# Gathers of later experts paced by the blocks of the expert in work

## The chip, the cores and the metric

The kernel runs on one core of a Trainium2 chip. The metric is the device time of one execution in microseconds (us); the smaller the better. Engines are named as in the profile: PE is TensorE (PEld its weight loads), DVE is VectorE, ACT is ScalarE, POOL is GpSimd, SP is SyncE, which issues the plain DMA transfers.

## What is computed

Attention with a local band of 96 keys and 8 global keys over q, k, v of shape (4, 8, 768, 64), then a mixture of eight experts in which each of the 3072 tokens goes to the one expert with the largest gate logit, with no token dropped:

```python
x = attn_out.transpose(0, 2, 1, 3).reshape(3072, 512)
logits = x @ w_gate                                # (3072, 8)
expert_idx = argmax(logits, axis=1)
gate_w = softmax(logits)[arange(N), expert_idx]
for e in range(8):
    lo, hi = boundaries[e], boundaries[e + 1]      # the tokens of expert e, sorted by expert
    h = maximum(x_sorted[lo:hi] @ w1[e], 0.0)      # w1[e]: 512 x 1024
    y_sorted[lo:hi] = h @ w2[e]                    # w2[e]: 1024 x 512
out = gate_w[:, None] * y_sorted[inv_perm]
```

All is float32.

## The kernel before

The first part, to about 230 us, is the attention, the gating and the sorting of tokens. It writes the attention's rows x into a DRAM tensor `x_tok` in pieces of 128 numbers. While it ends, the first 256 tokens of expert 0 are already worked on (`work`). Then each expert is worked on for as many tokens as its capacity says. The experts after 0 are taken in the order of their load, and position p below is the place in this order:

```python
CAPS = (464, 416, 416, 400, 400, 368, 368, 272)
ORDER = (0, 1, 2, 3, 4, 7, 5, 6)      # position 5 has capacity 272, positions 6 and 7 have 368
```

An expert's rows are brought from `x_tok` by indirect DMAs that GpSimd issues, one for 32 tokens (128 pieces of 512 bytes), into one of two buffers `xq_s`. VectorE then turns them in squares of 32 x 32, so that features lie along the partitions:

```python
def gather(xq, cols, n, top=N):
    for i in range(n):
        nc.gpsimd.indirect_dma_start(out=xq[:, i, :], out_offset=None, in_=x_tok[0:NJ * top, :],       # L261
                                     in_offset=bass.IndirectOffsetOnAxis(ap=cols[:, i:i + 1], axis=0), ...)

def turn_x(xe, xq, n):
    for i in range(n):
        nc.vector.transpose(xe[:, :, 32 * i:32 * i + 32], xq[:, i, :].rearrange("p (k q) -> p k q", k=KC))   # L268

def take(p):
    if p < E:
        r = ORDER[p] - 1
        xqs[p] = xq_s[p % 2]
        gather(xqs[p], rows_s[:, NQ * TB * r:NQ * TB * r + NQ * TB], pieces_of(CAPS[r + 1]))

def scaled(name, rows, po, gs, where, later=None):
    y = yp.tile([P, DM], F32, tag="y", name=name)
    nc.vector.tensor_scalar(out=y[0:rows, :], in0=po[0:rows, :], scalar1=gs[0:rows, :], ...)   # L287
    # then an indirect DMA that scatters y's rows to out (L279), at once or put on the list `later`
```

The end of the first part. `work(n)` does n pieces of expert 0's first two blocks of 128 tokens; the last four pieces are `result_0` of the second block and end in `scaled("y_0_1", ...)`. `fetch_0(1)` gathers expert 0's other tokens (seven gathers), `take(1)` those of position 1 (13 gathers):

```python
fetch_0(1)
settle()
work(1)
rows_of(ps_m, "_s", NR * NQ, st.pop(("w", 2)), rows_s)
take(1)
identify()
sort_acc(1, gslot_s)
fit()
work(3)
turn_x(xe_0, xq_0[0], TB)
work(4)
turn_x(xe_0[:, :, P:2 * P], xq_0[1], pieces_of(C0) - TB)
while later:
    later.pop(0)()          # the scatters of y_0_0 and y_0_1
```

The second part. Each position has a stage `hidden` (x times w1 and Relu, eight blocks fc of 128 hidden units, eight matmul instructions each) and a stage `result` (times w2, four blocks dc). `ph` has three PSUM buffers and `po` three. Each engine works in the order in which the program gives it its instructions:

```python
def fetch(p, i): ...        # SP: w1 (i = 0) or w2 (i = 1) of position p, 2 MB, into one of two buffers

def sort(p):                # VectorE
    xes[p] = xg.tile([P, KC, CM], F32, tag="xe", ...)
    turn_x(xes[p], xqs.pop(p), pieces_of(CAPS[ORDER[p]]))

def hidden(p, between=None):
    for fc in range(FC):
        ph = ps_h.tile([P, 512], F32, tag="ph", ...)
        for kc in range(KC):
            nc.tensor.matmul(ph[:, 0:C], lhsT=w1t[:, 0, kc, P * fc:P * fc + P], rhs=xe[:, kc, 0:C], ...)   # L1016
        nc.scalar.activation(hT[:, fc, 0:C], ph[:, 0:C], AF.Relu)                                          # L1018
        if fc == 0 and between:
            between()       # turns, scales and scatters the expert before (L1052, L287, L279)

def result(p):
    for dc in range(KC):
        po = ps_o.tile([P, DM], F32, tag="po", ...)
        for fc in range(FC):
            nc.tensor.matmul(po[:, 0:C], lhsT=w2t[:, 0, fc, P * dc:P * dc + P], rhs=hT[:, fc, 0:C], ...)   # L1043
        nc.vector.tensor_copy(out=yT[:, dc, 0:C], in_=po[:, 0:C])                                          # L1045
    return turn

fetch(1, 0)
fetch(1, 1)
ground()
sort(1)
take(2)
hidden(0)
turn = result(0)
...
for p in range(1, E):
    hidden(p, turn)
    fetch(p + 1, 0)
    sort(p + 1)
    take(p + 2)
    turn = result(p)
    fetch(p + 1, 1)
if turn:
    turn()
```

In position 0 this second part has only the 208 tokens (464 - 256) that `work` left.

Of the kernel before, what the change touches and what calls it, by code (L numbers as in the profile page):

```python
# [11 lines left out]
AF = mybir.ActivationFunctionType  # L12
# [4 lines left out]
P = 128  # L17
# [4 lines left out]
CAPS = (464, 416, 416, 400, 400, 368, 368, 272)  # L22
ORDER = (0, 1, 2, 3, 4, 7, 5, 6)
NQ = 4
# [5 lines left out]
def kernel(  # L30
# [12 lines left out]
    nc = tc.nc  # L43
# [3 lines left out]
    N = B * S  # L47
# [152 lines left out]
    def pieces_of(c):  # L200
        return (c + 31) // 32
# [50 lines left out]
    def rows_of(ps, nm, ns, mw, to_rows):  # L252
# [2 lines left out]
        nc.tensor.matmul(pw, lhsT=sel, rhs=mw.rearrange("p s g -> p (s g)"), start=True, stop=True)  # L255
        nc.vector.tensor_scalar(out=to_rows, in0=pw, scalar1=float(NJ), scalar2=j_of[:, 0:1], op0=ALU.mult, op1=ALU.add)

    def gather(xq, cols, n, top=N):

        for i in range(n):  # L260
            nc.gpsimd.indirect_dma_start(out=xq[:, i, :], out_offset=None, in_=x_tok[0:NJ * top, :],  # L261
                                         in_offset=bass.IndirectOffsetOnAxis(ap=cols[:, i:i + 1], axis=0),
                                         bounds_check=NJ * top - 1, oob_is_err=False)

    def turn_x(xe, xq, n):

        for i in range(n):
            nc.vector.transpose(xe[:, :, 32 * i:32 * i + 32], xq[:, i, :].rearrange("p (k q) -> p k q", k=KC))  # L268

    def take(p):  # L270
        if p < E:
            r = ORDER[p] - 1
            xqs[p] = xq_s[p % 2]
            gather(xqs[p], rows_s[:, NQ * TB * r:NQ * TB * r + NQ * TB], pieces_of(CAPS[r + 1]))

    scatters = []

# [49 lines left out]
    def banded_attention():  # L327
        with ExitStack() as actx:
# [317 lines left out]
            def work(pieces):  # L646

                for _ in range(pieces):
                    do, z, f0 = fill.pop(0)
                    do(z, f0)  # L650
# [139 lines left out]
            fit()  # L790
            work(3)
            turn_x(xe_0, xq_0[0], TB)
            work(4)
            turn_x(xe_0[:, :, P:2 * P], xq_0[1], pieces_of(C0) - TB)
            while later:
                later.pop(0)()

# [160 lines left out]

    with tc.manual_schedule():
        banded_attention()  # L960


        r2 = recips.rearrange("p a b -> p (a b)")
        bad = consts.tile([P, 1], F32)
        bad_i = consts.tile([P, 1], I32)

        def ground():
            okf = yp.tile([P, 2 * B * H * NB // 2], F32, tag="y", name="okf")
            nc.vector.tensor_scalar(out=okf, in0=r2, scalar1=R_MIN, scalar2=None, op0=ALU.is_ge)
            nc.vector.scalar_tensor_tensor(out=okf, in0=r2, scalar=R_MAX, in1=okf, op0=ALU.is_le, op1=ALU.mult)  # L970
            nc.vector.tensor_reduce(out=bad, in_=okf, axis=AX.X, op=ALU.min)
            nc.vector.scalar_tensor_tensor(out=bad, in0=ng, scalar=float(GW), in1=bad, op0=ALU.is_le, op1=ALU.mult)
            nc.vector.scalar_tensor_tensor(out=bad, in0=nl, scalar=float(LW), in1=bad, op0=ALU.is_le, op1=ALU.mult)
            nc.vector.scalar_tensor_tensor(out=bad, in0=nl, scalar=1.0, in1=bad, op0=ALU.is_ge, op1=ALU.mult)
            nc.vector.tensor_tensor(out=bad, in0=bad, in1=fits, op=ALU.mult)


        with ExitStack() as ectx:
            wp = ectx.enter_context(tc.tile_pool(name="wp", bufs=1))
            xg = ectx.enter_context(tc.tile_pool(name="xg", bufs=2))  # L980
            hp = ectx.enter_context(tc.tile_pool(name="hp", bufs=1))
            ps_h = ectx.enter_context(tc.tile_pool(name="ps_h", bufs=3, space=PSUM))
            ps_o = ectx.enter_context(tc.tile_pool(name="ps_oe", bufs=3, space=PSUM))
            ps_t = ectx.enter_context(tc.tile_pool(name="ps_te", bufs=2, space=PSUM))
            ws = [(w1_0, w2_0), (wp.tile([P, 1, KC, F], F32, name="w1_second"), wp.tile([P, 1, FC, DM], F32, name="w2_second"))]
            ids = {}
            xes, hTs = {0: xe_0}, {}

            def slots(p):
                return C0 if p == 0 else CAPS[ORDER[p]]  # L990

            def fetch(p, i):
                if p >= E:
                    return
                if p not in ids:
                    ids[p] = nc.values_load(ids_s[0:1, ORDER[p] - 1:ORDER[p]], engines=(mybir.EngineType.SP,),
                                            min_val=0, max_val=E - 1)
                if i == 0:
                    expert_w1(ws[p % 2][0], bass.ds(ids[p], 1))
                else:  # L1000
                    nc.sync.dma_start(ws[p % 2][1], w2v[:, bass.ds(ids[p], 1), :, :])

            def sort(p):
                if p < E:
                    xes[p] = xg.tile([P, KC, CM], F32, tag="xe", name=f"xe_{p}")
                    turn_x(xes[p], xqs.pop(p), pieces_of(CAPS[ORDER[p]]))

            def hidden(p, between=None):
                C = slots(p)
                w1t, xe = ws[p % 2][0], xes.pop(p)  # L1010
                hT = hp.tile([P, FC, CM], F32, tag="hT", name=f"hT_{p}")
                hTs[p] = hT
                for fc in range(FC):
                    ph = ps_h.tile([P, 512], F32, tag="ph", name=f"ph_{p}_{fc}")
                    for kc in range(KC):
                        nc.tensor.matmul(ph[:, 0:C], lhsT=w1t[:, 0, kc, P * fc:P * fc + P], rhs=xe[:, kc, 0:C],  # L1016
                                         start=(kc == 0), stop=(kc == KC - 1))
                    nc.scalar.activation(hT[:, fc, 0:C], ph[:, 0:C], AF.Relu)  # L1018
                    if fc == 0 and between:
                        between()  # L1020

            def finish(p, q, rows, po):
                r = ORDER[p] - 1
                g, i = (gslot_0[1][:, 0, :], idx_0[1][:, 0, :]) if p == 0 else (gslot_s[:, r, :], idx_s[:, r, :])
                scaled(f"y_{p}_{q}", rows, po, g[:, q:q + 1], i[:, q:q + 1])

            def result(p):

                C = slots(p)
                w2t, hT = ws[p % 2][1], hTs.pop(p)  # L1030
                if C % P == 0:
                    for q in range(C // P):
                        po = ps_o.tile([P, DM], F32, tag="po", name=f"po_{p}_{q}")
                        for fc in range(FC):
                            nc.tensor.matmul(po, lhsT=hT[:, fc, P * q:P * q + P], rhs=w2t[:, 0, fc, :],
                                             start=(fc == 0), stop=(fc == FC - 1))
                        finish(p, q, P, po)
                    return None
                yT = hp.tile([P, KC, CM], F32, tag="yT", name=f"yT_{p}")
                for dc in range(KC):  # L1040
                    po = ps_o.tile([P, DM], F32, tag="po", name=f"po_{p}_{dc}")
                    for fc in range(FC):
                        nc.tensor.matmul(po[:, 0:C], lhsT=w2t[:, 0, fc, P * dc:P * dc + P], rhs=hT[:, fc, 0:C],  # L1043
                                         start=(fc == 0), stop=(fc == FC - 1))
                    nc.vector.tensor_copy(out=yT[:, dc, 0:C], in_=po[:, 0:C])  # L1045

                def turn():
                    for o in range(0, C, P):
                        rows = min(P, C - o)
                        pt = ps_t.tile([P, DM], F32, tag="pt", name=f"pt_{p}_{o}")  # L1050
                        for dc in range(KC):
                            nc.tensor.transpose(pt[0:rows, P * dc:P * dc + P], yT[:, dc, o:o + rows], ident)  # L1052
                        finish(p, o // P, rows, pt)
                return turn

            fetch(1, 0)
            fetch(1, 1)
            ground()
            sort(1)
            take(2)  # L1060
            hidden(0)
            turn = result(0)
            pf = ps_t.tile([P, DM], F32, tag="pt", name="pf")
            nc.tensor.matmul(pf[:, 0:1], lhsT=ones, rhs=bad, start=True, stop=True)
            nc.vector.tensor_scalar(out=bad_i, in0=pf[:, 0:1], scalar1=P - 0.5, scalar2=None, op0=ALU.is_lt)
            for p in range(1, E):
                hidden(p, turn)
                fetch(p + 1, 0)
                sort(p + 1)
                take(p + 2)  # L1070
                turn = result(p)
                fetch(p + 1, 1)
            if turn:
                turn()
# [68 lines left out]
```

## Time and profile before

| what | value |
|---|---|
| time, median of 3 runs | 591.25 us (590.97 to 591.64) |
| span of the profiled execution | 589.4 us |
| PE busy | 532.9 us (90%), 3066 matmuls |
| PEld busy | 386.7 us (66%) |
| DVE busy | 205.5 us (35%) |
| POOL busy | 176.8 us (30%) |
| ACT busy | 101.4 us (17%) |
| gathers of L261 for positions 1 to 7 | 85, mean 1001 ns on POOL |
| weights, w1 or w2 of a position | 2 MB each, on the SP queue |

How to read it: a row of the timeline gives the start, the length, the engine, the line of the kernel, what is written and read, the number of instructions merged, and in square brackets how long the engine was idle before it and what is thought to have ended that wait. "remote", or "another core or an unknown queue", stands where no semaphore event on record explains it; "issue" stands where no wait is seen. On POOL a gather's row is the writing of its descriptors; when its rows land is not in it. The share of busy time is an average over stages: a stage is judged by what its last wait ends on.

### The profile page before, as it was taken

Reading aid. Unit: us, or ns where it says so; the run is one execution under the profiler, and the core shown is the slowest. Engines: PE = TensorE matmul, PEld = TensorE weight load, DVE = VectorE, ACT = ScalarE, POOL = GpSimd, SP = SyncE. Lnnn points to the kernel's source line nnn. Section 1 sums busy time; section 2 is a strip of 40 time slices with the busy share of each in tenths; the row PEclk is TensorE's granted clock in tenths of the full one; section 3 lists DMA queues with packets and bytes.
Section 4 is the critical chain, followed back from the end, with each engine's and each line's share of the span. In section 5 each row is a group of like instructions: output and inputs, shape, how many; then the busy total and the mean of one; then the engine's idle time right before and its main releaser. Section 6 shows DMA issues by size and latency. Waiting matters only on the chain.

```text
span 589.4 us, 8006 instructions
## 1 busy us (share of the span) xinstructions
PE 532.9 (90%) x3066; PEld 386.7 (66%) x3066; DVE 205.5 (35%) x537; ACT 101.4 (17%) x197; POOL 176.8 (30%) x227
## 2 busy tenths in 40 slices
PE   3999999999999985089999999999999969999993
PEld 2998988988988834087555555555555747666662
DVE  3886886876862533003003101301301302102011
ACT  2544334333332100010100100110110100100100
POOL 4332214231243077702701720710640640101001
PEclk9999999999999997579999999999999979999998
DMA  9999999999503087129173353562534737201001
GB/s 146 146 143 185 233 186 152 231 144 181 158 12 133 2 172 239 49 54 259 53 149 125 112 114 88 188 123 44 207 82 90 220 75 186 92 1 39 13 1 55
DMA packets 145184, 71.95 MB, mean 122 GB/s; under 512 B 126656, under 2 KB 126660, under 8 KB 145136
## 3 DMA queue, kind: packets, MB, share of 16 engines
q1 hardware_dynamic: 137344, 58.16, 47.4%
q0 software_dynamic: 5264, 12.59, 6.7%
q10 hardware_dynamic: 2528, 0.59, 0.7%
q8 instruction: 26, 0.43, 0.3%
q14 instruction: 22, 0.18, 0.1%
HBM read 59.00 MB, written 12.65 MB: 122 GB/s over the span
## 4 chain that ended last, share of the span: by engine, by line
PE 75%; another core or an unknown queue 11%; DVE 5%; DMA 3%; SPq 2%; issue 1%; ACT 1%; POOL 1%; ACTq 0%; POOLq 0%; DVEq 0%
PE po L1043 26%; PE ph L1016 24%; PE o L495 10%; PE s L463 7%; PE ph L298 3%; PE px L511 2%; PE pt L1052 2%; SPq L362 2%; DMA vt<-in_v_dram 1%; DVE y L287 1%; PE pi L603 1%; PE pq L526 1%; DMA x_tok<-xr 1%; PE pl L539 1%
## 5 line engine op out<-in xcount | busy, mean ns | idle before, releaser
L1045 DVE COPY yT<-po 128x416 f32<-128x416 f32 (+4 forms) x32 | 16.9, 529 | 280.9 <-PE po L1043 280.9
L1016 PE MATMUL ph<-xe,w_first 128*128 128x208 f32 (+3 forms) x256 | 80.8, 477 | 25.5 <-ACT hT L1018 18.7
L261 POOL DMA_INDIRECT xq_s<-x_tok,rows_s x85 | 85.1, 1001 | 25.9 <-issue 24.4
L1043 PE MATMUL po<-hT,w_second 128*128 128x416 f32 (+3 forms) x256 | 81.2, 478 | 5.6 <-ACT hT L1018 5.6
L1016 PEld LDWEIGHTS ph<-xe,w_first 128*128 128x128 f32 x256 | 51.1, 204 | 53.5 <-ACT hT L1018 19.3
L1018 ACT ACTIVATE hT<-ph 128x416 f32<-128x416 f32 (+4 forms) x64 | 29.8, 467 | 324.9 <-PE ph L1016 212.9
L279 POOL DMA_INDIRECT out_dram<-y,idx_s x25 | 24.2, 969 | 204.3 <-DVE y L287 200.9
L1016 PE MATMUL ph<-xe,w_second 128*128 128x416 f32 (+3 forms) x256 | 79.7, 470 | 0.0
L1043 PE MATMUL po<-hT,w_first 128*128 128x208 f32 (+3 forms) x256 | 75.5, 456 | 0.0
L1043 PEld LDWEIGHTS po<-hT,w_second 128*128 128x128 f32 x256 | 49.5, 194 | 36.7 <-issue 10.2
L495 PE MATMUL o<-vt,e 128*128 128x128 f32 x384 | 72.1, 276 | 0.0
L1016 PEld LDWEIGHTS ph<-xe,w_second 128*128 128x128 f32 x256 | 48.3, 190 | 28.6 <-issue 9.8
L1043 PEld LDWEIGHTS po<-hT,w_first 128*128 128x128 f32 x256 | 47.8, 190 | 27.1 <-issue 10.0
L495 PE MATMUL o<-va,e 128*128 128x128 f32 x320 | 62.7, 278 | 0.0
L466 ACT ACTIVATE e<-s 128x1024 f32<-128x1024 f32 (+1 forms) x48 | 45.6, 951 | 94.3 <-issue 47.3
L495 PEld LDWEIGHTS o<-vt,e 128*128 128x128 f32 x384 | 57.0, 192 | 1.5 <-issue 1.0
L477 DVE TENSOR_TENSOR e<-e,Wb 128x512 f32<-128x512 f32 x64 | 45.3, 750 | 15.4 <-ACT e L466 15.2
L495 PEld LDWEIGHTS o<-va,e 128*128 128x128 f32 x320 | 48.5, 192 | 2.6 <-issue 2.5
L463 PE MATMUL s<-qT,kT 64*128 64x128 f32 x384 | 40.7, 290 | 0.9 <-ACT qT L397 0.9
L463 PE MATMUL s<-qT,kA 64*128 64x128 f32 x320 | 35.6, 300 | 3.6 <-POOL kA L381 3.6
L463 PEld LDWEIGHTS s<-qT,kT 64*128 64x128 f32 x384 | 30.8, 196 | 2.8 <-ACT qT L397 1.3
L405 POOL COPY va<-vt 128x650 f32<-128x650 f32 x16 | 14.6, 913 | 57.1 <-DMA vt<-in_v_dram 46.8
(163 smaller groups left out, 433.7 us busy)
## 6 DMA issues: line engine op xcount, KB each, us to landing
w_second<-in_moe_w_dram SPq DMA_DIRECT2D x16, 512.0 KB, 9.5
w_second<-in_moe_w_dram SPq DMA_DIRECT2D x4, 2048.0 KB
x_tok<-xr SPq DMA_DIRECT2D x24, 256.0 KB, 3.5
w_first<-in_moe_w_dram SPq DMA_DIRECT2D x12, 512.0 KB, 7.7
w_first<-in_moe_w_dram SPq DMA_DIRECT2D x3, 2048.0 KB
vt<-in_v_dram SPq DMA_DIRECT2D x31, 192.0 KB, 4.7
qb<-in_q_dram SPq DMA_DIRECT2D x60, 96.0 KB, 4.3
kb<-in_k_dram SPq DMA_DIRECT2D x60, 96.0 KB, 3.7
```

Source lines behind the costliest of these rows:

```text
L261: nc.gpsimd.indirect_dma_start(out=xq[:, i, :], out_offset=None, in_=x_tok[0:NJ * top, :], in_offset=bass.IndirectOffsetOnAxis(ap=cols[:, ...
L279: p = nc.gpsimd.indirect_dma_start(out=out[:, :], out_offset=bass.IndirectOffsetOnAxis(ap=where, axis=0), in_=y[0:rows, :], in_offset=None ...
L298: nc.tensor.matmul(ph[:, P * f:P * f + P], lhsT=w1_0[:, 0, kc, c0:c0 + P], rhs=xe_0[:, kc, P * q:P * q + P], start=(kc == 0), stop=(kc == ...
L405: nc.gpsimd.tensor_copy(out=to, in_=vh[:, :, 0:VA])
L463: nc.tensor.matmul(ps[:, h, P * m:P * m + P], lhsT=lhsT, rhs=qT[r, P * i:P * i + P], start=True, stop=True)
L466: nc.scalar.activation(e[:, :, 0:w], ps[:, :, 0:w], AF.Exp, scale=D ** -0.5)
L477: nc.vector.tensor_tensor(out=eh, in0=eh, in1=W[:, 2 * j + h, P:3 * P].rearrange("p (o c) -> p o c", o=1).to_broadcast([P, 2, 2 * P]), op= ...
L495: nc.tensor.matmul(po[:, t, h, :], lhsT=pt[:, h, P * m:P * m + P], rhs=(vt if own else va)[:, c0:c0 + P], start=(m == mine[0][0]), stop=(m ...
L1016: nc.tensor.matmul(ph[:, 0:C], lhsT=w1t[:, 0, kc, P * fc:P * fc + P], rhs=xe[:, kc, 0:C], start=(kc == 0), stop=(kc == KC - 1))
L1018: nc.scalar.activation(hT[:, fc, 0:C], ph[:, 0:C], AF.Relu)
L1043: nc.tensor.matmul(po[:, 0:C], lhsT=w2t[:, 0, fc, P * dc:P * dc + P], rhs=hT[:, fc, 0:C], start=(fc == 0), stop=(fc == FC - 1))
L1045: nc.vector.tensor_copy(out=yT[:, dc, 0:C], in_=po[:, 0:C])
```

## The change

The 13, 12 or 9 gathers of a position are no longer issued in one run. `plan(p)` only lists them. `pace(n, after)` takes up to n from the list and makes each wait for the instruction `after`: one after each of the first seven Relus of the stage in work, what is left after the eighth, two after the first copy of a result stage and one after each of the other three. So the gathers for position 2 start in result(0) and end with hidden(1), where they all stood ahead of hidden(0) before; those of position p + 2 start in result(p) and end with hidden(p + 1). `take(1)` stays as it was. The aim is that gathers never come in long runs beside the experts' blocks. The second part of the change has VectorE turn the last three pieces of expert 0's rows before it scales `y_0_1`, so that hidden(0) need not wait for that scaling. No matmul, transfer or byte is added or taken away.

```diff
@@ -255,23 +255,42 @@
         nc.tensor.matmul(pw, lhsT=sel, rhs=mw.rearrange("p s g -> p (s g)"), start=True, stop=True)
         nc.vector.tensor_scalar(out=to_rows, in0=pw, scalar1=float(NJ), scalar2=j_of[:, 0:1], op0=ALU.mult, op1=ALU.add)
+    def gather_one(xq, cols, i, top=N):
+
+        return nc.gpsimd.indirect_dma_start(out=xq[:, i, :], out_offset=None, in_=x_tok[0:NJ * top, :],
+                                            in_offset=bass.IndirectOffsetOnAxis(ap=cols[:, i:i + 1], axis=0),
+                                            bounds_check=NJ * top - 1, oob_is_err=False)
+
     def gather(xq, cols, n, top=N):
-
         for i in range(n):
-            nc.gpsimd.indirect_dma_start(out=xq[:, i, :], out_offset=None, in_=x_tok[0:NJ * top, :],
-                                         in_offset=bass.IndirectOffsetOnAxis(ap=cols[:, i:i + 1], axis=0),
-                                         bounds_check=NJ * top - 1, oob_is_err=False)
+            gather_one(xq, cols, i, top)
     def turn_x(xe, xq, n):
         for i in range(n):
             nc.vector.transpose(xe[:, :, 32 * i:32 * i + 32], xq[:, i, :].rearrange("p (k q) -> p k q", k=KC))
-    def take(p):
+    pending = []
+
+    def plan(p):
         if p < E:
             r = ORDER[p] - 1
             xqs[p] = xq_s[p % 2]
-            gather(xqs[p], rows_s[:, NQ * TB * r:NQ * TB * r + NQ * TB], pieces_of(CAPS[r + 1]))
+            cols = rows_s[:, NQ * TB * r:NQ * TB * r + NQ * TB]
+            for i in range(pieces_of(CAPS[r + 1])):
+                pending.append((xqs[p], cols, i))
+
+    def pace(n, after):
+
+        for _ in range(min(n, len(pending))):
+            g = gather_one(*pending.pop(0))
+            tc.add_manual_dep(g.ins, after.ins.name, mybir.DependencyInfo(mybir.DependencyClass.Sync, mybir.DependencyReason.DATA),
+                              reason="spreads the gathers over the experts' work")
+
+    def take(p):
+        plan(p)
+        while pending:
+            gather_one(*pending.pop(0))
     scatters = []
@@ -790,8 +809,8 @@
             fit()
             work(3)
             turn_x(xe_0, xq_0[0], TB)
+            turn_x(xe_0[:, :, P:2 * P], xq_0[1], pieces_of(C0) - TB)
             work(4)
-            turn_x(xe_0[:, :, P:2 * P], xq_0[1], pieces_of(C0) - TB)
             while later:
                 later.pop(0)()
@@ -1015,9 +1034,10 @@
                     for kc in range(KC):
                         nc.tensor.matmul(ph[:, 0:C], lhsT=w1t[:, 0, kc, P * fc:P * fc + P], rhs=xe[:, kc, 0:C],
                                          start=(kc == 0), stop=(kc == KC - 1))
-                    nc.scalar.activation(hT[:, fc, 0:C], ph[:, 0:C], AF.Relu)
+                    done = nc.scalar.activation(hT[:, fc, 0:C], ph[:, 0:C], AF.Relu)
                     if fc == 0 and between:
                         between()
+                    pace(1 if fc < FC - 1 else len(pending), done)
             def finish(p, q, rows, po):
                 r = ORDER[p] - 1
@@ -1042,7 +1062,7 @@
                     for fc in range(FC):
                         nc.tensor.matmul(po[:, 0:C], lhsT=w2t[:, 0, fc, P * dc:P * dc + P], rhs=hT[:, fc, 0:C],
                                          start=(fc == 0), stop=(fc == FC - 1))
-                    nc.vector.tensor_copy(out=yT[:, dc, 0:C], in_=po[:, 0:C])
+                    pace(2 if dc == 0 else 1, nc.vector.tensor_copy(out=yT[:, dc, 0:C], in_=po[:, 0:C]))
                 def turn():
                     for o in range(0, C, P):
@@ -1057,8 +1077,8 @@
             fetch(1, 1)
             ground()
             sort(1)
-            take(2)
             hidden(0)
+            plan(2)
             turn = result(0)
             pf = ps_t.tile([P, DM], F32, tag="pt", name="pf")
             nc.tensor.matmul(pf[:, 0:1], lhsT=ones, rhs=bad, start=True, stop=True)
@@ -1067,7 +1087,7 @@
                 hidden(p, turn)
                 fetch(p + 1, 0)
                 sort(p + 1)
-                take(p + 2)
+                plan(p + 2)
                 turn = result(p)
                 fetch(p + 1, 1)
             if turn:
```

## The prediction

> **What bounds the kernel now.** I read the chain of work that ended last first, because it says which engine sets the end. From 272 us on it is nearly all matmuls, 22 us of L1016 and 22 us of L1043 for each large expert. The long foreign pieces lie around expert 0 (columns: start, us, what); shorter ones of 3 to 5 us stand at 466 to 482:
> ```profile
> 204.62 26.46 another core or an unknown queue
> 231.09 0.03 ACTq L1018
> ...
> 231.58 20.54 another core or an unknown queue
> 252.11 0.02 issue
> 252.14 0.35 ACT hT L1018
> ...
> 252.53 7.85 PE ph L1016 x32
> 260.38 11.25 PE po L1043 x64
> ```
> The reader is to see 47 us in which ScalarE waits for something that the chain cannot name, just ahead of the first two Relus of expert 0. I then put the stretches side by side (length; PE, PEld, DVE, ACT, POOL busy with counts; granted clock, DMA share, GB/s):
> ```profile
> 225.00:235.00 10.00, 5.69 (x26) 4.77 (x24) 2.88 (x10) 0.34 (x1) 7.56 (x9) 0.84 0.62 220
> 235.00:245.00 10.00, 0.00 (x0) 0.00 (x0) 0.00 (x0) 0.00 (x0) 7.77 (x8) 0.50 0.18 52
> 245.00:252.60 7.60, 0.07 (x1) 0.07 (x1) 0.00 (x0) 0.34 (x1) 3.99 (x4) 0.50 0.15 42
> ```
> From 235 to 245 nothing works but GpSimd, which issues gathers; the DMA engines are at 0.18, so no transfer is short of bandwidth. Third, the timeline of the same place:
> ```profile
> 222.36 6.14 PE L1016 MATMUL ph<-xe,w_first 128*128 128x208 f32 x24 [3.64 <-issue]
> 231.23 0.34 ACT L1018 ACTIVATE hT<-ph 128x208 f32<-128x208 f32 x1 [26.71 <-remote]
> 231.63 2.19 PE L1016 MATMUL ph<-xe,w_first 128*128 128x208 f32 x8 [3.13 <-issue]
> 249.11 1.00 POOL L261 DMA_INDIRECT xq_s<-x_tok,rows_s  x1 [0.30 <-issue]
> 252.14 0.34 ACT L1018 ACTIVATE hT<-ph 128x208 f32<-128x208 f32 x1 [20.56 <-remote]
> 252.53 7.85 PE L1016 MATMUL ph<-xe,w_first 128*128 128x208 f32 x32 [18.71 <-ACT hT L1018]
> ```
> TensorE had done three blocks of eight matmuls by 228.5 us, all three ph buffers were full, and it stood. The Relu of block 1, whose matmuls the records end at 227.1, began at 252.14: 2.0 us after the end of the last gather of take(2), 249.11 + 1.00 = 250.11. Nothing that this Relu reads or writes belongs to a gather. So word from TensorE reaches ScalarE late while gathers run back to back. I checked this on all 64 Relus, by the end of the last matmul of each block in the single records: 0.04 to 0.10 us is the normal step, and only in the later part of a run of gathers is it longer, 5.8, 25.1, 25.8, 20.7 us (expert 0), up to 3.7 (position 2), 1.4 (3), 3.0 (4), and in position 5:
> ```profile
> 469.13 0.40 ACT L1018 ACTIVATE hT<-ph 128x272 f32<-128x272 f32 x1 [3.07 <-remote]
> 472.71 0.40 ACT L1018 ACTIVATE hT<-ph 128x272 f32<-128x272 f32 x1 [3.18 <-remote]
> 477.69 0.40 ACT L1018 ACTIVATE hT<-ph 128x272 f32<-128x272 f32 x1 [4.58 <-remote]
> 481.94 0.40 ACT L1018 ACTIVATE hT<-ph 128x272 f32<-128x272 f32 x1 [3.86 <-remote]
> ```
> Their matmuls ended at 467.5, 469.3, 471.1 and 473.0, so they are 1.7, 3.4, 6.6 and 9.0 us late. The gathers ran from 464.17 to 479.53. In positions 6 and 7, where nothing is gathered, every step is 0.04 to 0.10 us.
>
> **What the Trainium skill says.** "Perfetto Trace Analysis", section "DMA Instruction — SWDGE (GPSIMD)": the recorded end of such an instruction is the last descriptor written, not the data's arrival. "DMA: Bandwidth & Descriptors", section "Anatomy of one DMA — SWDGE (gpsimd) path": about 2.0 us of fixed cost per DMA, most of it the wait for the write receipt. The trace agrees: late Relus are let go 2.0 to 2.5 us after the last gather's recorded end (250.11 to 252.14; 479.53 to 481.94). "Perfetto Trace Analysis", section "Tensor Engine Instruction (MATMUL, LD_WEIGHTS)": a matmul's end is estimated and the semaphore is pushed once PSUM has acknowledged; so lateness counted from that end is a reading, though 0.04 us in quiet stretches speaks for it. "TensorE: Matmul & The Clock Gate", Part 1: an idle array falls to half clock and needs about 3.4 us of work to come back; the trace shows 0.50 in 235–245. No page that I found says why TensorE's semaphores should come late under gathers; I take that as an observation.
>
> **The change part by part.**
> 1. Take(2), 13 gathers at 1.30 us between 233.45 and 250.11, leaves its place ahead of hidden(0). Hidden(0) then has no gathers of its own; what is left beside it is take(1), 213.91 to 230.52, and the two scatters of expert 0's early rows, to 233.14. Hidden(0) now lasts 222.36 to 260.38 = 38.0 us. Its 64 matmuls of 208 columns need 11.25 us (the 64 of the same shape in result(0) take that). If block 0 is let go at 231.2 as now, TensorE does block 3 by 233.8. Block 1's Relu should come 2.0 to 2.4 us after the last gather or scatter, 232.5 to 235.5, and then four blocks of 1.41 us remain, with 1.5 us for half clock: an end at about 240 to 242.6. If the three early blocks are let go sooner, five blocks follow 228.5 without a pause: 235.5. So 18 to 25 us less; I take 20.
> 2. The spread gathers: five in each result (after the copies of L1045, 5.6 us apart for 416 columns, 2.8 us in result(0)) and the rest in the next hidden, one a block (2.79 us for 416 columns, 1.83 us for 272). The count stays 85. Issued at half the density or less, they should rarely make TensorE's word late; and as each now waits for a Relu or a copy, a late word holds back the next gather, so lateness cannot pile up. In positions 2, 3 and 4 that gains nothing, since the PE row has no pause there: three ph buffers cover 3 us. In position 5 TensorE stands 2.4 us (475.7 to 478.1) and 3.2 us (479.2 to 482.4), then runs at half clock. Result(5) takes 472.8 to 495.5 = 22.7 us where 64 x 0.229 = 14.7 would do: 8.0 us lost. But hidden(5) is short: four scatters and seven gathers in 15 us are still close together. I take 6 of the 8.
> 3. The last three transposes for expert 0 ahead of y_0_1. They are to save the 0.75 us of L287 and the wait for result_0 before it. But two of them waited for their gathers, not for VectorE:
> ```profile
> 220.97 0.31 DVE L268 STREAM_TRANSPOSE xe<-xq 128x128 f32<-128x128 f32 x1 [0.93 <-DMA xq<-x_tok,rows]
> 221.90 0.31 DVE L268 STREAM_TRANSPOSE xe<-xq 128x128 f32<-128x128 f32 x1 [0.61 <-DMA xq<-x_tok,rows]
> ```
> Those rows landed about 8 us after issue, beside expert 1's weights (DMA share 1.03 in 215–225). Hidden(0) cannot start before 222.2. I count 0.
> 4. Added: a semaphore wait per gather, on an engine busy 30%. I count 0.
>
> Sum: 591.25 - 20 - 6 = 565.
>
> **Rivals.**
> (a) The late word is no matter of the gathers' density but of any gather in flight. Then position 5 gains nothing and other blocks lag 2 to 3 us, which three buffers hide; hidden(0) still gains, as it has no gathers after 233. About 571 to 574. For it: late words occur at one gather per 1.3 us with little DMA traffic. Against: the first 8 to 15 us of each run of gathers are undisturbed, and position 1 takes 13 gathers with no late Relu.
> (b) Gathers become the bound: they end one hidden later, beside the weight loads, so sort(p+1), and VectorE's copies behind it, wait. The last gather of an expert is issued after the last Relu of the hidden before; with the 8 us of landing seen above it is there 9 us later. The copies of L1045 then slip 3 to 5 us, which three po buffers cover, and the rows are needed only a result later (22 us, 14.7 for position 5). No cost, unless landing takes over 14 us; if it did, 2 to 5 us for each of six experts, 575 to 590.
> (c) Block 0's lateness comes from take(1), which stays, and the gap drags on longer than to 235. Then hidden(0) ends nearer 247 and the time is about 572.
> (d) All lateness goes: 25 + 8, so 558.
>
> **Range and chances.** 565 is steps 1 and 2. The low end, 556, is (d) with a little for half clock regained; the high end, 574, is (a) or (c). Within 2% means above 579.4 us, for which take(2)'s burst would have to hurt as much elsewhere: 0.04. Slower needs (b) in its worst form: 0.01.
>
> **What would show it.** Right: hidden(0) free of a TensorE pause after about 236 us, its last matmul at 235 to 243; single gathers 2.8 to 5.6 us apart; Relus within 0.1 us of their blocks in positions 1 to 4; result(5) in 15 to 17 us; and the start of hidden(0) unmoved near 222.3 (step 3). Wrong: Relus of expert 0 still released only with a later gather, or VectorE's copies waiting for gathers long enough to stop TensorE.

## The result and the profile after

| | us, median | range | runs |
|---|---|---|---|
| before | 591.44 | 590.97 to 593.37 | 4 |
| after | 569.11 | 566.92 to 575.23 | 4 |

The ratio is 0.9633, with a 95% interval of 0.9556 to 0.971. The span of the profiled execution fell from 589.4 to 566.7 us. In the changed kernel the gather is L260, the scaling L306, the scatter L298, the matmul of hidden L1035, its Relu L1037, the matmul of result L1063 and its copy L1065.

From the two pages first: TensorE's row of 40 slices, before and after, and the chain that ended last in the changed kernel, by engine.
```profile
PE   3999999999999985089999999999999969999993
...
PE   3999999999999997499999999999999998999993
...
PE 45%; issue 25%; POOL 10%; DMA 9%; DVE 6%; SPq 2%; another core or an unknown queue 2%; POOLq 1%; ACTq 0%; ACT 0%; DVEq 0%
```
TensorE did the same 3066 matmuls; at expert 0 its row fell to 5 and 0 before and falls to 4 now, at position 5 to 6 before and to 8 now, and "another core or an unknown queue", 11% of the chain before, is 2%. The 25% of "issue" and 10% of POOL are a trap. A gather now waits for a Relu, so the chain can be followed back through gathers and the time between two Relus; TensorE was busy 529.4 us (93% of the span, 90% before) all the same, and its row shows where time is lost.

The timeline of the changed kernel at hidden(0), picked from ScalarE, TensorE and GpSimd:
```profile
221.30 5.87 PE L1035 MATMUL ph<-xe,w_first 128*128 128x208 f32 x32 [3.43 <-DVE xe L271]
223.10 0.34 ACT L1037 ACTIVATE hT<-ph 128x208 f32<-128x208 f32 x1 [19.43 <-DMA w_second<-in_moe_w_dram]
231.34 1.01 POOL L298 DMA_INDIRECT out_dram<-y,idx  x1 [0.31 <-issue]
235.04 0.81 ACT L1037 ACTIVATE hT<-ph 128x208 f32<-128x208 f32 x3 [11.59 <-remote]
235.43 8.15 PE L1035 MATMUL ph<-xe,w_first 128*128 128x208 f32 x32 [8.27 <-ACT hT L1037]
```
Block 0's Relu is on time, then three Relus come together at 235.04, 2.7 us after the end of the last scatter of the old run (231.34 + 1.01 = 232.35). TensorE stands 8.27 us here, where it stood 3.13 and 18.71. Hidden(0) ends at 243.6 where it ended at 260.38 before. No gather runs beside it after 229.7; the next one, at 247.15, waits for a copy of result(0).

Position 5 of the changed kernel:
```profile
455.01 0.69 ACT L1037 ACTIVATE hT<-ph 128x272 f32<-128x272 f32 x2 [3.81 <-PE ph L1035]
456.20 1.95 SPq L241 DMA_DIRECT2D w_second<-in_moe_w_dram  x4
456.98 1.00 POOL L260 DMA_INDIRECT xq_s<-x_tok,rows_s  x1 [0.30 <-issue]
468.28 0.31 DVE L271 STREAM_TRANSPOSE xe<-xq_s 128x128 f32<-128x128 f32 x1 [5.97 <-DMA xq_s<-x_tok,rows_s]
468.51 1.10 DVE L1065 COPY yT<-po 128x272 f32<-128x272 f32 x3
468.97 3.93 PE L1063 MATMUL po<-hT,w_second 128*128 128x272 f32 x16 [1.80 <-DVE yT L1065]
```
The two Relus at 455.01 are 2.5 and 1.0 us late. TensorE does not wait for them itself, but the gathers that hang on them do: the last one goes at 456.98, behind SyncE's issue of the next weights at 456.20, and shares the DMA engines with them (share 1.02 from 457 to 467). Its rows are turned at 468.28, three copies of result(5) stand behind that in VectorE's order, and the fourth block finds no free po buffer: a new wait of 1.80 us. Result(5) takes 456.00 to 472.90 = 16.9 us, 22.7 before.

So of the 22.7 us by which the span is shorter, 16.8 are gone by the end of hidden(0) (0.85 of them because the attention part was that much earlier in this execution: its first gather of `fetch_0(1)` came at 203.91, before at 204.76), and 495.5 - 472.9 = 22.6 by the end of result(5).

### The profile page after: what moved, and what is told of

Its sections match the earlier page's. It is cut to its first block, busy times and chain, and to the rows that moved or that the text cites. A ratio compares the mean times of both kernels' runs of the same rounds, so it can differ in the third digit from the quotient of the medians.

```text
span 566.7 us, 8069 instructions
## 1 busy us (share of the span) xinstructions
PE 529.4 (93%) x3066; PEld 384.9 (68%) x3066; DVE 209.0 (37%) x537; ACT 101.2 (18%) x197; POOL 177.3 (31%) x227
## 3 DMA queue, kind: packets, MB, share of 16 engines
q0 software_dynamic: 5264, 12.59, 7.1%
## 4 chain that ended last, share of the span: by engine, by line
PE 45%; issue 25%; POOL 10%; DMA 9%; DVE 6%; SPq 2%; another core or an unknown queue 2%; POOLq 1%; ACTq 0%; ACT 0%; DVEq 0%
PE o L514 11%; PE po L1063 10%; PE ph L1035 9%; POOL xq_s L260 8%; PE s L482 7%; DMA xq_s<-x_tok,rows_s 3%; PE ph L317 3%; PE px L530 2%; DMA w_second<-in_moe_w_dram 2%; SPq L381 2%; POOL out_dram L298 1%; PE pi L622 1%; DMA vt<-in_v_dram 1%; PE pq L545 1%
## 5 line engine op out<-in xcount | busy, mean ns | idle before, releaser
L260 POOL DMA_INDIRECT xq_s<-x_tok,rows_s x85 | 85.4, 1004 | 155.4 <-DVE yT L1065 104.8
L1035 PE MATMUL ph<-xe,w_first 128*128 128x208 f32 (+3 forms) x256 | 78.6, 467 | 11.7 <-ACT hT L1037 8.3
L1037 ACT ACTIVATE hT<-ph 128x416 f32<-128x416 f32 (+4 forms) x64 | 29.6, 468 | 303.3 <-PE ph L1035 255.8
L1063 PE MATMUL po<-hT,w_second 128*128 128x416 f32 (+3 forms) x256 | 79.2, 469 | 1.8 <-DVE yT L1065 1.8
L1035 PE MATMUL ph<-xe,w_second 128*128 128x416 f32 (+3 forms) x256 | 79.7, 469 | 0.0
L1035 PEld LDWEIGHTS ph<-xe,w_first 128*128 128x128 f32 x256 | 49.5, 198 | 39.1 <-issue 14.1
L1063 PE MATMUL po<-hT,w_first 128*128 128x208 f32 (+3 forms) x256 | 75.5, 456 | 0.0
L1063 PEld LDWEIGHTS po<-hT,w_second 128*128 128x128 f32 x256 | 48.6, 190 | 31.8 <-issue 10.2
L271 DVE STREAM_TRANSPOSE xe<-xq_s 128x128 f32<-128x128 f32 x85 | 23.5, 296 | 126.4 <-DMA xq_s<-x_tok,rows_s 119.4
L1035 PEld LDWEIGHTS ph<-xe,w_second 128*128 128x128 f32 x256 | 48.3, 190 | 28.7 <-issue 9.9
L1063 PEld LDWEIGHTS po<-hT,w_first 128*128 128x128 f32 x256 | 47.7, 190 | 27.1 <-issue 10.2
L1065 DVE COPY yT<-po 128x416 f32<-128x416 f32 (+4 forms) x32 | 16.3, 522 | 132.7 <-PE po L1063 132.7
L298 POOL DMA_INDIRECT out_dram<-y,idx_s x25 | 24.3, 971 | 75.9 <-DVE y L306 72.5
```

The costliest lines, as they stand in the source:

```text
L260: return nc.gpsimd.indirect_dma_start(out=xq[:, i, :], out_offset=None, in_=x_tok[0:NJ * top, :], in_offset=bass.IndirectOffsetOnAxis(ap=c ...
L298: p = nc.gpsimd.indirect_dma_start(out=out[:, :], out_offset=bass.IndirectOffsetOnAxis(ap=where, axis=0), in_=y[0:rows, :], in_offset=None ...
L1037: done = nc.scalar.activation(hT[:, fc, 0:C], ph[:, 0:C], AF.Relu)
L1065: pace(2 if dc == 0 else 1, nc.vector.tensor_copy(out=yT[:, dc, 0:C], in_=po[:, 0:C]))
```

## The experiments

Theory A is the prediction's: TensorE's word (the semaphore signal by which another engine learns that TensorE's work is done) comes late while indirect DMAs follow each other at 1.3 us; thin them out and it doesn't. Rival R1: any gather in flight makes it late, and the change helps by moving gathers. Rival R2: the gain is from the order of work, the waits or the earlier transposes, and late words are a side show. "Lateness" is, as in the prediction, the start of a Relu less the modelled end of its block's last matmul.

The runs came in six sets; five of them were on five different chips, the chip of the result isn't known. The kernel before takes 591 to 595 us in four sets and 558 to 559 us in two, so every ratio below is against the kernel before in the same set. I call the chips of the first kind late and of the second quiet; late 1 is the chip of the result.

| run | chip | this, us | before, us | ratio, 95% interval |
|---|---|---|---|---|
| e1_one_run_after_hidden0 | quiet 1 | 558.57 | 558.16 | 1.0015 [0.9993, 1.0038] |
| e2_position2_as_before | quiet 1 | 558.12 | 558.16 | 1.002 [1.0001, 1.0039] |
| e3_transposes_as_before | quiet 1 | 558.51 | 558.16 | 1.0012 [0.9997, 1.0027] |
| e5_position1_paced | quiet 1 | 558.28 | 558.16 | 1.0016 [0.9987, 1.0044] |
| p1_changed_again | late 2 | 571.20 | 592.39 | 0.9646 [0.9565, 0.9727] |
| f2_wider_spaced | late 3 | 572.72 | 594.63 | 0.9631 [0.9584, 0.9677] |
| g1_one_run_after_hidden0 | late 3 | 586.19 | 594.63 | 0.9857 [0.978, 0.9934] |
| f1_plain_dma_gpsimd | late 4 | 572.80 | 592.45 | 0.966 [0.9565, 0.9754] |
| f1s_plain_dma_sp | late 4 | 572.15 | 592.45 | 0.9649 [0.9569, 0.9729] |
| g5_position1_paced | late 4 | 563.12 | 592.45 | 0.9497 [0.9418, 0.9575] |
| h1_half_rows | quiet 2 | 560.51 | 558.71 | 1.0029 [1.0006, 1.0052] |
| g2_position2_as_before | quiet 2 | 558.31 | 558.71 | 0.9996 [0.998, 1.0012] |

### Parts of the change, on a quiet chip

e1: the changed kernel, but position 2's gathers in one run behind the last Relu of hidden(0), and those of later positions in one run each, as before.
```diff
-                    pace(1 if fc < FC - 1 else len(pending), done)
+                    if p == 0 and fc == FC - 1:
+                        pace(len(pending), done)
...
-                    pace(2 if dc == 0 else 1, nc.vector.tensor_copy(out=yT[:, dc, 0:C], in_=po[:, 0:C]))
+                    nc.vector.tensor_copy(out=yT[:, dc, 0:C], in_=po[:, 0:C])
...
+            plan(2)
             hidden(0)
-            plan(2)
...
-                plan(p + 2)
+                take(p + 2)
```


> All gathers stay in runs as in the kernel before; only the run of 13 for position 2 is held back until the last Relu of hidden(0). If the gain in position 0 comes from that one move and the gain in position 5 from the spread, this takes most of step 1 and none of step 2: position 0 as in the changed kernel (hidden(0) over at about 244 us), result(5) still 22 to 23 us, so about 591.3 - 17 = 574 to 576 us. If the late words come with any gather in flight near a stage, 13 gathers beside result(0) cost there what they cost before and the time is 585 to 591 us.

e2: the changed kernel, but `take(2)` in one run ahead of hidden(0), as before.
```diff
+            take(2)
             hidden(0)
-            plan(2)
```


> The changed kernel, but with the 13 gathers for position 2 in one run ahead of hidden(0), as before. If steps 1 and 2 are independent, hidden(0) ends at about 260 us again, result(5) stays at 16 to 17 us, and the time is 591.3 - 6 = 584 to 586 us. If the spread of the later gathers is what frees position 0 too, the time is near 569 us.

e3: the changed kernel without its second part (the last three transposes behind `work(4)` again).
```diff
-            turn_x(xe_0[:, :, P:2 * P], xq_0[1], pieces_of(C0) - TB)
             work(4)
+            turn_x(xe_0[:, :, P:2 * P], xq_0[1], pieces_of(C0) - TB)
```


> The changed kernel with the last three transposes for expert 0 behind the scaling of y_0_1 again. If these transposes wait for their gathers (my step 3), the time is within 0.5 us of the changed kernel, 568 to 570 us. If they waited for VectorE, hidden(0) starts up to 3 us later and the time is 571 to 572 us.

e5: the changed kernel, and `take(1)` thinned out too: eight gathers at once, the other five behind the Relus of blocks 3 to 6 of hidden(0); `sort(1)` and the two early scatters behind hidden(0).
```diff
-            take(1)
+            plan(1)
+            for _ in range(8):
+                gather_one(*pending.pop(0))
...
-            while later:
-                later.pop(0)()
+            held.extend(later)
...
+                    if p == 0:
+                        pace({3: 2, 4: 1, 5: 1, 6: 1}.get(fc, 0), done)
...
-            sort(1)
             hidden(0)
+            sort(1)
+            while held:
+                held.pop(0)()
             plan(2)
```


> The changed kernel, but of the 13 gathers for position 1 only eight are issued at once; five wait for the Relus of blocks 3 to 6 of hidden(0), and the two scatters of expert 0's early rows follow them. If what still holds three Relus of hidden(0) until 235 us is the run of gathers and scatters that lasts to 232.4 us, they go 2.0 to 2.7 us after the eighth gather, at about 225 to 226 us, TensorE hardly stops and hidden(0) ends at 233 to 235 us instead of 243.6: 559 to 561 us. If those Relus wait for something else that is over at about 235 us (weights, the release of the attention's tiles), the time stays at 567 to 570 us.

All four lie within 0.2% of the kernel before, so none met the times expected for it; every difference that lateness was to make is missing. Their traces say why: no Relu is over 0.16 us late in any of them, runs of gathers or not. The one that should have hurt, e2, in its timeline:
```profile
221.64 12.95 PE L1035 MATMUL ph<-xe,w_first 128*128 128x208 f32 x64 [3.11 <-DVE xe L271]
...
234.62 1.01 POOL L260 DMA_INDIRECT xq_s<-x_tok,rows_s  x1 [0.30 <-issue]
234.63 0.34 ACT L1037 ACTIVATE hT<-ph 128x208 f32<-128x208 f32 x1 [1.06 <-PE ph L1035]
```
GpSimd is in the same run of gathers and scatters, 1.30 us apart, as in the kernel before on the late chip. Here all 64 matmuls of hidden(0) stand in one unbroken row, and the last Relu begins 0.04 us after them. This speaks against R2: without late words the order of work, the added waits and the earlier transposes are worth nothing that can be measured. It also sizes the whole of the lateness: 591.4 on the late chip less 558.2 here is 33 us. The kernel before was only timed here, not profiled, but by stages e2 comes to the same: hidden(0) takes 12.95 us where the kernel before took 38.0 on the late chip, and result(5) 14.83 where it took 22.7, 33 us together.

e3 speaks on step 3 directly. With the transposes behind the scaling again, in e3:
```profile
218.25 0.75 DVE L306 TENSOR_SCALAR y<-po,gslot 128x512 f32<-128x512 f32 x1 [3.83 <-PE po L324]
219.88 0.31 DVE L271 STREAM_TRANSPOSE xe<-xq 128x128 f32<-128x128 f32 x1 [0.57 <-DMA xq<-x_tok,rows]
220.79 0.31 DVE L271 STREAM_TRANSPOSE xe<-xq 128x128 f32<-128x128 f32 x1 [0.61 <-DMA xq<-x_tok,rows]
```
The last two wait for their rows, whether the scaling is ahead of them or not.

### The same on late chips

p1: the changed kernel once more, nothing edited.

> The changed kernel once more. Four variants and the kernel before all took 558 us in the last runs, and none of their Relus was late, though e2 had the run of 13 gathers beside hidden(0). If late words are a condition of the chip that some chips show and others don't, then beside a kernel before at about 558 us this takes 557 to 560 us with no late Relu, and beside one at about 591 us it takes 567 to 571 us. If the program decides, the ratio to the kernel before is 0.96 wherever it runs.

0.9646, as the first time. The Relus of blocks 1 to 3 of hidden(0) are 7.9, 6.6 and 5.5 us late, in positions 1 to 4 all are within 0.10 us, in position 5 at most 1.8 us late. But result(5) has no pause here. In p1:
```profile
458.62 14.83 PE L1063 MATMUL po<-hT,w_second 128*128 128x272 f32 x64
459.09 1.00 POOL L260 DMA_INDIRECT xq_s<-x_tok,rows_s  x1 [0.49 <-ACT hT L1037]
459.88 1.85 SPq L241 DMA_DIRECT2D w_second<-in_moe_w_dram  x4
```
The last gather goes 0.8 us ahead of the weights, and its rows are turned 3.7 us after its issue; in the result's execution it went 0.8 us behind them, and 11.3 us passed. e3, with no late Relu, has the first order (447.47, weights at 448.37): 3.1 us and no pause. g5, below, has the second (452.09, weights at 451.25): 10.0 us and a pause of 0.58 us. So the pause in result(5) comes of the late Relus by way of the gather, and not in every execution. The four executions agree on this; no run changes that order alone.

f2: the kernel before, with a fill of 1.5 us on GpSimd ahead of each gather of positions 2 to 7. The gathers keep their place, wait for nothing, and are as many; they only come 2.67 us apart.
```diff
-            gather(xqs[p], rows_s[:, NQ * TB * r:NQ * TB * r + NQ * TB], pieces_of(CAPS[r + 1]))
+            cols = rows_s[:, NQ * TB * r:NQ * TB * r + NQ * TB]
+            for i in range(pieces_of(CAPS[r + 1])):
+                if p > 1:
+                    nc.gpsimd.memset(idle, 0.0)          # 128 x 1664
+                gather(xqs[p][:, i:i + 1, :], cols[:, i:i + 1], 1)
```


> The kernel before, with a memset of 128 x 1664 numbers on GpSimd (1.47 us in the trace of before) ahead of each gather of positions 2 to 7: the same gathers in the same places, but about 2.8 us apart instead of 1.3, and waiting for no Relu. On a chip where the kernel before takes about 591 us: if the density of gathers makes TensorE's word late, the Relus of expert 0 and of position 5 come on time and the time is 565 to 572 us; if any gather in flight does it, the now longer row of 13 gathers holds expert 0 even longer and the time is 591 to 605 us. On a chip where it takes about 558 us, 558 to 560 us.

In the timeline of f2, at hidden(0) and in position 5:
```profile
236.15 1.05 POOL L262 DMA_INDIRECT xq_s<-x_tok,rows_s  x1 [0.17 <-issue]
237.20 1.51 POOL L278 MEMSET idle<- 128x1664 f32 x1
238.87 1.02 POOL L262 DMA_INDIRECT xq_s<-x_tok,rows_s  x1 [0.17 <-issue]
...
243.15 0.34 ACT L1023 ACTIVATE hT<-ph 128x208 f32<-128x208 f32 x1 [2.22 <-PE ph L1021]
...
460.76 14.83 PE L1048 MATMUL po<-hT,w_second 128*128 128x272 f32 x64
```
While `take(1)` and the scatters go by at 1.3 us, the first Relus are 9.7, 11.3 and 10.6 us late; the fourth, due at 238.9, is 1.7. The last of them go 5 us after the last scatter, not 2 to 3 as elsewhere; why is not known. From there on every Relu of the kernel is within 0.10 us, though gathers at 2.67 us run on beside hidden(0) and result(0). Result(5) is 14.83 us of matmuls without a pause. The gain, 0.9631 [0.9584, 0.9677], is that of the change, without its waits and its order. (572.72 us is 0.7 above the range expected, which had not allowed for the late Relus under `take(1)`.) That fells R1: gathers in flight don't do it, gathers in close order do. Nor does GpSimd's being busy: with the fills it worked 31.6 of the 34 us from 236 to 270.

g1: e1 again, on this chip. If gains simply add, it should keep step 1's and lose step 2's.

> The kernel of e1 once more: all gathers in runs, but the run for position 2 held back until the last Relu of hidden(0). On a chip where the kernel before takes about 591 us and the changed one about 570: if the gains of the two parts add, hidden(0) is over at about 244 us, position 5 keeps its late Relus, and the time is 574 to 577 us. If the run hurts result(0) as it hurt hidden(0), 585 to 591 us. On a chip of 558 us, 558 us again.

It gained only 8.4 us (0.9857), within the 585 to 591 us expected if the run hurts what it now stands beside. Hidden(0) does end early, at 246.6; but the run of 13 gathers, moved behind it (247.25 to 263.97), now meets result(0) and hidden(1). In g1's timeline:
```profile
262.35 0.38 DVE L1066 COPY yT<-po 128x208 f32<-128x208 f32 x1 [6.08 <-PE pt L1073]
...
262.97 1.00 POOL L260 DMA_INDIRECT xq_s<-x_tok,rows_s  x1 [0.30 <-issue]
...
266.04 0.52 ACT L1037 ACTIVATE hT<-ph 128x416 f32<-128x416 f32 x1 [19.06 <-remote]
```
The last copy of result(0), whose matmuls were over at 257.9, starts at 262.35: VectorE gets TensorE's word late as well. The first Relu of hidden(1), due at 260.9, is 5.2 us late. Moving a run doesn't remove its harm; it hits what stands beside it then. In position 5 the lateness is the old one, 1.7, 3.4, 7.3 and 9.0 us.

f1 and f1s: the kernel before, where the gathers of positions 2 to 7 are plain DMAs of the same size, 128 rows of 512 bytes, issued by GpSimd (f1) or by SyncE (f1s). They leave out the choice of rows by index: each takes rows that follow each other.
```diff
...                                                     # p == 1: gather(...) as before
+            else:
+                for i in range(pieces_of(CAPS[r + 1])):
+                    nc.gpsimd.dma_start(xqs[p][:, i, :], x_tok[P * i:P * i + P, :])     # f1s: nc.sync
```


> The kernel before, but positions 2 to 7 get their rows by plain DMAs of 128 rows of 512 bytes that GpSimd issues in the same place and number; the choice of rows by index is left out, so these rows are not the tokens' own. On a chip where the kernel before takes about 592 us: if many DMAs issued by GpSimd in a row make TensorE's word late, whatever their addresses, the late Relus of expert 0 and position 5 stay and the time is 585 to 595 us; if it takes indirect ones, 560 to 566 us. On a chip of 558 us, 556 to 559 us.

> As f1, but the same plain DMAs are issued by SP, so that their descriptors come from the hardware queue; bytes, number and completions are the same. On a chip where the kernel before takes about 592 us: if it is the landing of many small DMAs (their completions, 16 each) that delays TensorE's word, the late Relus stay, 580 to 595 us; if it is GpSimd's part in them, no Relu after take(1) is late and the time is 558 to 566 us. On a chip of 558 us, 556 to 562 us.

f1 at hidden(0):
```profile
239.22 1.00 POOL L283 DMA_INDIRECT out_dram<-y,idx  x1 [0.31 <-issue]
240.21 7.00 POOL L278 DMA_DIRECT2D xq_s<-x_tok  x13
242.89 0.81 ACT L1022 ACTIVATE hT<-ph 128x208 f32<-128x208 f32 x3 [11.04 <-remote]
```
Thirteen plain DMAs, 0.54 us each on the same engine and thus denser than the gathers, let the Relus go at 242.89 in the midst of them, 2.7 us after the last scatter; hidden(0) goes on, and in positions 1 to 7 no Relu is over 0.10 us late. f1s is the same. So it is indirect DMAs that do it, not GpSimd's transfers as such nor their number; nor the number of packets, as GpSimd's queue moved 5264 in f1 and in the kernel before. One reserve: f1's run is over in 7.0 us, where 13 gathers take 16.7, so a longer run of plain DMAs by GpSimd stays untried; 13 by SyncE take 13.8 us in f1s, without harm. f1 is 6.8 us and f1s 6.2 us above the range expected; what the expectations missed is the run of `take(1)` and the scatters, which both keep (9.2, 8.1 and 6.9 us late), and in f1's profiled execution an attention part some 6 us longer. What in an indirect DMA does it, its descriptors, its index reads or its completions, is open.

g5: e5 on a late chip.

> The kernel of e5 once more: the changed kernel with the gathers for position 1 broken up as well (eight at once, five behind Relus of hidden(0), the two early scatters after them). On a chip where the kernel before takes about 592 us and the changed one 570: if the three late Relus of hidden(0) come from the run of 22 gathers and scatters, hidden(0) ends 7 to 9 us earlier and the time is 561 to 564 us; if they come from something else, 568 to 572 us. On a chip of 558 us, 558 us again.

In g5:
```profile
222.93 14.50 PE L1037 MATMUL ph<-xe,w_first 128*128 128x208 f32 x64 [3.06 <-issue]
```
The 8.27 us pause of hidden(0) is gone: 64 matmuls in one row, 14.50 us. The run of 22 gathers and scatters was what held the three Relus, and the time is within the 561 to 564 us expected. This version is the best of the study: 563.12 us, 0.9497 [0.9418, 0.9575] of the kernel before on this chip, and no slower than it on the quiet one (1.0016).

### Two runs that met a quiet chip

h1: the kernel before, each gather of positions 2 to 7 of 64 rows instead of 128 (half of the rows are left out), with a short fill ahead. It was to tell the number of rows from the number of instructions.
```diff
+                    nc.gpsimd.memset(idle, 0.0)          # 128 x 512
...
-  out=xq[:, i, :],        ... ap=cols[:, i:i + 1]
+  out=xqs[p][0:64, i, :], ... ap=cols[0:64, i:i + 1]
```


> The kernel before, but each gather of positions 2 to 7 fetches 64 rows in place of 128 (half of the rows are left out), and a fill of 128 x 512 on GpSimd stands ahead of each, so that the gathers start about as far apart as before, 1.3 to 1.6 us; they wait for nothing. If it is the number of row descriptors in a given time that makes TensorE's word late (98 rows per us before, 48 in the run with 128 rows 2.67 us apart, which had no late word), 64 rows per 1.3 us is 49 per us: no Relu late through the run of take(2), 570 to 574, late Relus of hidden(0) only until take(1)'s run is over. If it is the number of indirect instructions in a given time, whatever they fetch, the Relus of hidden(0) stay late until the run of take(2) is over, 20 us and more, and those of position 5 by 2 to 9 us: 588 to 595. On a chip that shows no late Relu in the kernel before, it tells nothing.

g2: e2 once more, to see whether the two gains add.

> The kernel after, but take(2) in one run ahead of hidden(0) as in the kernel before; the gathers of the later experts stay spread. On a chip that shows late Relus: if the two gains of the prediction add, only step 2's share is left, 5 to 6 us: ratio 0.990, about 585 to 587 beside 592, with hidden(0) 36 to 38 us long. If, as the run with position 2 alone moved suggests, each half of the change does less alone than in company, the ratio is above 0.995. On a chip that shows none: 1.000 to 1.003.

Neither has a Relu over 0.16 us late, so neither tells what it was for. g2 repeats what the first quiet chip showed: to spread the later gathers is worth nothing there (0.9996). Whether step 2 alone is worth its 6 us on a late chip, and whether rows or instructions count, was thus not found out.

## Why the prediction was right, step by step

**The bound and the mechanism** held: late words from TensorE, made by indirect DMAs in close order (f2, with f1 for "indirect"), and not the order of work (f2 on a late chip, e1 to e3 on the quiet one). Of its signs of being right, no pause of TensorE after 236 us, the Relus of positions 1 to 4 and result(5) came as named. What it could not know is that this depends on the chip: its 565 holds for late chips alone.

**Step 1**, 20 us: measured 16.8, and 16 without the shift of the attention part. The mechanism was right and the size off. Block 0 was let go at 223.10, not at 231.2, which gained nothing, since the next three Relus waited until 235.04, the late end of "232.5 to 235.5". Then came four blocks as reckoned, but at half clock for longer: 8.15 us, where I had 4 x 1.41 + 1.5 = 7.1. The granted clock is 0.50 from 235.43 to 240.0, 4.6 us; in the kernel before it had been 4.0 us after the pause, and the same four blocks took 7.85 us there, in a line that the prediction shows. Both are longer than the 3.4 us that the prediction cites; what is measured holds. The end, 243.6, lies past "240 to 242.6". And it was not enough that take(2) left its place: in g1 it did so as one run, and all that was gained is 8.4 us.

**Step 2**, 6 us: measured 5.8 (22.6 - 16.8), result(5) 16.9 us long. I left 2 us for words still late, and about 2 are lost, but by a way that I had not seen: not TensorE waiting for a Relu, but a late Relu that held a gather back behind the weights, and the gather VectorE's copies. That the size fits is in part luck: in p1 result(5) took 14.83 us, which is all of the 8.

**Step 3**, 0: right. Hidden(0) began 1.06 us earlier, 0.85 of which is the attention part's; e3 shows the wait for the rows. But the two lines there do not say "about 8 us after issue": their gathers went at 211.32 and 212.62, so it was 9.7 and 9.3 us.

**Step 4**, 0: right, by e1 to e5 on the quiet chip, all within 0.2%.

**Rival (a)** is out by f2. **Rival (c)** is what is left of hidden(0)'s loss, milder than I had it (243.6, not 247), and g5 removes it. **Rival (d)**, 25 + 8 = 33 us, is just the distance of the late chip from the quiet one, and g5 comes within 5 us of it. **Rival (b)** was seen for the rows of positions 2, 3, 4 and 6, and one step of its dismissal failed. For position 2's rows, beside result(1) of the changed kernel:
```profile
279.11 0.99 POOL L260 DMA_INDIRECT xq_s<-x_tok,rows_s  x1 [1.80 <-ACT hT L1037]
288.91 0.31 DVE L271 STREAM_TRANSPOSE xe<-xq_s 128x128 f32<-128x128 f32 x1 [9.77 <-DMA xq_s<-x_tok,rows_s]
289.15 1.05 DVE L1065 COPY yT<-po 128x416 f32<-128x416 f32 x2
```
The last rows are turned 9.8 us after the gather's issue, near the 9 us I reckoned, and the copies slip by 5 us for free. But "no cost, unless landing takes over 14 us" took the length of result(5) as the limit. The limit is three po buffers: 48 matmuls of 272 columns are 11.2 us, and in position 5 the rows took 468.28 - 456.98 = 11.3 from issue. That is the prediction's own second sign of being wrong, VectorE's copies stopping TensorE, seen in one of the two profiled executions of the changed kernel and at 1.80 us. (Rival (b) in its worst form also adds up to 577 to 595, not 575 to 590: 565 and six times 2 to 5 us.) The copies bunched in this way also release gathers 1.3 us apart (289.97, 291.27), against "2.8 to 5.6 us apart".

**"The trace agrees"** sets two spans side by side that are not the same: the fixed cost of a DMA, and the time from a gather's recorded end until a late Relu goes. The last rows of `take(1)` in the kernel before, issued at 229.52, were turned at 232.04, 2.5 us after the issue and 1.5 after the recorded end; late Relus go 2.0 to 2.9 us after such an end. That they wait for the last landing is not shown.

**Open**: why TensorE's words come late under close indirect DMAs, what in these does it, and why on some chips only. No chip is known to have been met twice, so chip and hour are not told apart. That a word is late between a matmul's end and its arrival is read from modelled ends; that it is TensorE's words in particular, and that thinning cures it, is what the runs show.

## What to carry to other kernels

If an engine waits for nothing that the profile can name while GpSimd issues indirect DMAs back to back, set the lateness of that engine's starts beside the run of gathers; if it grows along the run and ends a few us after it, space the gathers out by giving each a block of the work to wait for, as moving the run only moves the harm. Hang the last of them early enough that they go ahead of the next big transfer, and that the rows land before the PSUM buffers behind the consumer's queue are used up, here within 11 us of the stage's start. Measure on more than one chip: in two sets of six nothing was left of this gain of 4 to 5%.

## What was not expected of the hardware

- The same kernel took 591 to 595 us in four sets of runs and 558 to 559 in two, each steady within about 1%. What sets them apart in the traces is words that come up to 25.8 us late on the first and, in six traces of its variants, never over 0.16 us late on the second.
- It goes one way. In the run of gathers of the kernel before, where TensorE's words were 6.6 us late, ScalarE's word reached TensorE at once: a Relu ending at 477.69 + 0.40 = 478.09 was followed by TensorE at 478.14. The gathers' own words came in time as well: the last rows of `take(1)`, issued at 229.52, were turned at 232.04, while the Relu due at 227.1 waited until 252.14.
- The trace's own records of landings in GpSimd's DMA queue go missing with it: 514 in the kernel before and 1150 in the changed one, 2060 to 2062 in the four runs on the first quiet chip, for the same 129 indirect DMAs. Whether the two have one cause is open.
- A gather of 64 rows holds GpSimd 0.95 us, one of 128 rows 1.00 us: half of the rows save 0.05 us of the issue.
